# Attention with a small state and a gated MLP on one core: x of batch 0 in 2 KB pieces, its state read in 64x32 tiles in one visit

## The chip, the core and the metric

The kernel runs on one core of a Trainium2 chip. The metric is the device time of one execution in microseconds (us). The core's engines run side by side and meet only at semaphores: TensorE (PE in the profile, with its weight loads as PEld), VectorE (DVE), ScalarE (ACT), GpSimd (POOL) and SyncE (SP), whose queue issues nearly all transfers here. 16 DMA engines move the bytes.

## The reference

`x` is [8, 8, 512, 64] (batch, head, token, feature) and `state` is [8, 8, 32, 64], all in float32. Tokens read from the state, the state reads from the tokens, and both results go through one MLP:

```
scores  = x @ state^T / 8;  a  = softmax(scores)       # over the 32 states
xread   = a @ state                                    # 512 rows of a head
scores2 = state @ x^T / 8;  a2 = softmax(scores2)      # over the 512 tokens
sread   = a2 @ x                                       # 32 rows of a head
attn    = concat([xread, sread], rows)                 # 544 rows of a head
X       = heads side by side                           # [8 * 544, 512]
out     = mish(X @ w_in) @ w_out                       # 512 -> 2048 -> 512
```

In the code the state read (`sread`) is the product of the exponentials `e2` with x; `rs` holds the reciprocals of their sums.

## The kernel before, in words

The weights are loaded as 32-bit words, put together and split into a high and a low float32r part; the products of the MLP are sums of three float32r matmuls. `w_in` is folded with the state of a batch first (`sw`, psum `swp`), so that the attention's read and the first layer are one product (`ph`). Mish of it is `g`, split into `gh` and `gl`, and the second layer accumulates in `acc`.

Batch 0 is the prologue. While the weights still arrive, its attention, the preparation of all weights and its MLP are interleaved by a list of steps that is written out by hand. Each step is a generator: every mention in the list runs it up to its next `yield`, so one step has two or three parts on different engines. PE, DVE and ACT each execute their instructions in the order of that list. Afterwards the batches 1 to 7 run in a loop of eight slots each, with the attention of the next batch in between; there DVE and ACT are ordered by the planner, and PE still in the order of the code.

The transfers go out on SP's queue in program order, mostly chained behind one another: the four pieces of x of batch 0 first (256 KB each, a pair of heads, line 124), then `w_in` and `w_out` by turns (`wir`, line 173, and `wor`, line 185). The state of batch 0 (`sn`) goes out on ACT's queue at the same time.

These steps of the list carry what follows (all of batch 0, all recorded under line 66, the helper that issues them):

- `x0` to `x3`: four PE transposes of a pair of heads into a bank (`xTp`), then a copy to SBUF (`xT`), by ACT for pairs 0 and 2, by DVE for 1 and 3. `st` (psum `st`) transposes the state on PE by products with the identity, `sc` makes the scores, `scs` their scaled copy.
- `tr`, `ex`, `no`, `pr`: the softmax over the states, up to `ah` and `al`, the operands of the first layer. `p0` to `p7` are the first layer's products, `m0` to `m7` their Mish on ACT and the split on DVE, `g0` to `g7` the second layer.
- `hi`, `ci`, `di`, `ji` put the words of `w_in` together, `ho`, `co`, `do`, `jo`, `lo` those of `w_out`, on ACT and DVE; `sw0` to `sw7` fold `w_in` on PE (`swp`), copied to `swh` by ACT and `swl` by DVE.
- `ee0`, `ee1`: the exponentials `e2` of the two halves of the heads (a half is one head of each pair, kc = 0 or 1; 128 rows are 4 heads x 32 states), first on ACT, then the sums' reciprocals on DVE.
- `et0`, `et1`: the first part is on PE, four transposes of 128x128 of half kc into a bank `e2p`; the second is on ACT, the copy to `e2T`.
- `sr0`, `sr1`: the first part is on PE, 16 float32 matmuls for half kc (four token groups x four heads, each 128 tokens deep, 32 states by 64 features) into a bank `srp`; the second is on DVE, the scaling to `srd`.

The order around them is this stretch of the list; between the first parts of `et1` and `sr0` there is no other PE work, and on ACT the Mish of `m3` is ahead of the second part of `et1`:

```
... sw3 ee0 g1 g1 sw3 et0 m2 ee1 ci4 co3 sw3 et0 p3
m2 jo2 et1 lg2 lo2 m3 et1 sr0 ho3 g2 ji4 sw4 ho5 sr0 g2 g2 g2 sr1 jo3 sw4 ... sr1 p4
```

`e2p`, `srp`, `swp` and `xTp` share the two banks of the pool `misc`. A float32 matmul that isn't a transpose is executed as two passes, and the profile counts both.

Of the kernel before, what the change touches and what calls it, by code (L numbers as in the profile page):

```python
# [9 lines left out]
F32 = mybir.dt.float32  # L10
# [7 lines left out]
P = 128  # L18
B, H, S, NS, D = 8, 8, 512, 32, 64
# [29 lines left out]
def half(par):  # L49
    return slice(par * D, (par + 1) * D)  # L50
# [23 lines left out]
def state_attention_mish_kernel(ctx, tc, x, state, w_in, w_out, out):  # L74
# [11 lines left out]
    def misc(name):  # L86
        return ps_m.tile([P, 512], F32, tag="m", name=name)

    def spare(b):


        return misc if b < 2 else first_bank
# [7 lines left out]
    def temp(name, shape=(P, S)):  # L100
        return pool.tile(list(shape), F32, tag="t", name=name, bufs=5)
# [13 lines left out]

    def load_x(b):

        shape = [P, NC, 2, NT * D]
        if b == 0:
            xs = const.tile(shape, F32, tag="wo7", name="x_0")  # L120
        else:
            xs = pool.tile(shape, F32, tag="x", name=f"x_{b}", bufs=1)
        for c in range(NC):
            last["load"] = nc.sync.dma_start(  # L124
                xs[:, c], x[b].rearrange("(c k) (p t) d -> c p k (t d)", k=2, t=NT)[c])
        return xs
# [129 lines left out]
    def attention(b, sn, xq=None):  # L256
# [4 lines left out]
        def x_transposed(c):  # L261

            if xq is not None:
                xTs[c] = temp(f"xT_{b}_{c}")
                dve.transpose(
                    xTs[c].rearrange("p (k v i g) -> p g k v i", k=2, v=2, g=4),
                    xq[:, c].rearrange("p k (g v) d -> p g k v d", v=2))
                return
            pt = (first_bank if b == 0 and c > 1 else misc)(f"xTp_{b}_{c}")
            for i in range(NT):  # L270
                pe.transpose(
                    pt[:, i * P:(i + 1) * P], xss[b][:, c, i // 2, (i % 2) * P:(i % 2 + 1) * P], ident)
            yield
            xTs[c] = temp(f"xT_{b}_{c}")
            if b == 0 and c % 2:
                dve.tensor_copy(xTs[c], pt)
            else:
                act.copy(xTs[c], pt)

        def scores():  # L280

# [39 lines left out]
        def soft2_e(kc):  # L321
            e2 = temp(f"e2_{b}_{kc}")
            sm = pool.tile([P, 1], F32, tag="sm", name=f"sm_{b}_{kc}")
            act.activation(e2, sc[kc], AF.Exp, bias=nms[kc], accum_out=sm)
            yield
            dve.tensor_scalar_add(sm, sm, 1e-9)
            rs2[kc] = pool.tile([P, 1], F32, tag="rs", name=f"rs_{b}_{kc}", bufs=4)
            dve.reciprocal(rs2[kc], sm)
            e2s[kc] = e2

        def e2_transposed(kc):
            e2 = e2s[kc]
# [49 lines left out]
        def soft1_n():  # L382
            sums, turned = ([small[kc][i] for kc in two] for i in (1, 2))

            def total(kc):
                dve.tensor_reduce(sums[kc], groups(e1[kc]), AX.X, ALU.add)

            def guard(kc):
                dve.tensor_scalar_add(sums[kc], sums[kc], 1e-9)

            def turn(kc):
                dve.reciprocal(turned[kc], sums[kc])

            def norm(kc):
                dve.tensor_mul(groups(e1[kc]), groups(e1[kc]), wide(turned[kc]))

            for step, kc in ((total, 0), (guard, 0), (total, 1), (turn, 0), (guard, 1), (norm, 0)):
                step(kc)
            yield
            turn(1)  # L400
            norm(1)
# [21 lines left out]

        def sread(kc):

            if b == 0 or kc == 0:
                srd["bank"] = misc(f"srp_{b}_{kc}") if b == 0 else spare(2)(f"srp_{b}")
            pr = srd["bank"][:, :D] if b == 0 else srd["bank"][:, kc * D:(kc + 1) * D]
            for t in range(NT):
                for h4 in range(4):  # L430
                    o = slice(h4 * NS, (h4 + 1) * NS)
                    last["PE"] = pe.matmul(
                        pr[o],
                        e2T[kc][:, t, o],
                        xss[b][:, h4, kc, t * D:(t + 1) * D],
                        start=(t == 0), stop=(t == NT - 1),
                    )
            yield
            if kc == 0 and b == 0:
                srd[0] = pool.tile([P, 2, D], F32, tag="srd", name=f"srd_{b}", bufs=1)  # L440
            dve.tensor_scalar_mul((srds[0][:, b - 1] if b else srd[0])[:, kc], pr, rs2[kc])

        def sreadT():
            pt = misc(f"srTp_{b}")[:, :P]
# [7 lines left out]

        own = dict(
            x=x_transposed, st=lambda _: state_blocks(b, sn) if b else state_blocks_0(sn), sc=lambda _: scores(), tr=soft1_t, ex=soft1_x,
            no=lambda _: soft1_n(), pr=soft1_a, mm=soft2_m, ee=soft2_e, et=e2_transposed, sr=sread,
            rt=lambda _: sreadT(), fill=fill, aT=aT)

        def soft2():
# [114 lines left out]
    def gemm2(key, fcs, gh, gl, ntok, ts=None):  # L573

        if key not in accs:
            new_accs(key, ntok)
        for t in ts or range(ntok):

            parts = (slice(0, 256), slice(256, 512)) if (key, fcs[-1], t) == (B - 1, NFC - 1, ntok - 1) else (slice(0, 512),)
            for part in parts:  # L580
                for i, fc in enumerate(fcs):
                    col = (i * ntok + t) * P
                    sl = slice(col, col + P)
                    ops = [(gh, 1), (gh, 0), (gl, 1)]
                    for n, (g, w) in enumerate(ops):
                        last["PE"] = pe.matmul(
                            accs[key][t][:, part], g[:, sl], wo[fc // 2][:, fc % 2, w, part],
                            start=(fc == 0 and n == 0), stop=(fc == NFC - 1 and n == 2),
                            skip_group_check=part.start > 0,
                        )  # L590
            if len(parts) > 1:
                for part, engine in zip(parts, (act.copy, dve.tensor_copy)):
                    o = pool.tile([P, 256], F32, tag="e2T", name=f"o_{key}_{t}_{part.start}")
                    engine(o, accs[key][t][:, part])
                    (nc.scalar if part.start else nc.sync).dma_start(
                        out[key * T:key * T + S, part].rearrange("(p t) e -> p t e", t=NT)[:, t, :], o)
            elif fcs[-1] == NFC - 1:
                o = pool.tile([P, DM], F32, tag="o", name=f"o_{key}_{t}")
                if t % 2 == 0:
                    dve.tensor_copy(o, accs[key][t])  # L600
                else:
                    act.copy(o, accs[key][t])
                if key == "s":
                    for b4 in range(4):
                        r0 = (4 * t + b4) * T + S
                        nc.sync.dma_start(out[r0:r0 + NS, :], o[b4 * NS:(b4 + 1) * NS, :])
                else:
                    last["store"] = nc.sync.dma_start(
                        out[key * T:key * T + S, :].rearrange("(p t) e -> p t e", t=NT)[:, t, :], o)


    raws, rawo, wfull = {}, {}, {}
# [62 lines left out]
    for step in """  # L675
            x0 x0 x1 x1 st st x2 x2 x3 x3 sc acc sc sc sc sc ci0 tr0 tr1 hi0 tr0 tr0 ex0 tr1 tr1 fill2
            ex1 ci1 ji0 sw0 no sw0 sw0 fill2 no hi1 pr0 ho0 pr0 ji1 pr1 pr1 co0 fill2 pr0 pr1 sw1 jo0
            sw1 p0
            m0 ho1 fill6 jo0 sw1 hi2 m0 lo0 lg0 p1
            do1 di2 ji2 jo1 g0 g0 sw2 mm0 m1 hi4 sw2 hi3 jo1 g0 sw2 ci3 lo1 m1 lg1 g0 p2  # L680
            g1 ji3 g1 ho2 mm1 do2 jo2 ee0 ee1 sw3 ee0 g1 g1 sw3 et0 m2 ee1 ci4 co3 sw3 et0 p3
            m2 jo2 et1 lg2 lo2 m3 et1 sr0 ho3 g2 ji4 sw4 ho5 sr0 g2 g2 g2 sr1 jo3 sw4 m3 sw4 jo3 ci5 ho4
            hi5 hi6 co5 lo3 sr1 p4
            co4 ji5 sw5 sw5 lg3 ST g3 m4 sw5 g3 jo4 X1 jo4 p5
            lo4 rt X1 X2 ci6 g3 rt m4 ji6 lg4 X0 rt X2 m5 X0 X3 sw6 X3 jo5 jo5 sw6 co6 lo5 g3 SC g4 sw6
            m5 SC lg5 SC TR0 ho6 TR0 g4 p6
            EX0 TR1 TR1 g4 jo6 g4 ci7 hi7 EX1 ji7 g5 g5 ho7 m6 sw7 jo6 sw7 NO NO g5 sw7 m6 PR0 g5 next
            p7
            lo6 lg6 co7 g6 next g6 m7 next jo7 PR1 PR1 jo7 PR0 g6 m7 PR1 PR0 lo7 lg7 g6
            """.split():  # L690
        what, i = re.fullmatch(r"([a-zA-Z]+)(\d*)", step).groups()
        if not hasattr(begun.get(step), "send"):
            begun[step] = steps[what](int(i or 0))
        if hasattr(begun[step], "send"):
            next(begun[step], None)
# [123 lines left out]
```

## Time and profile before

| what | value |
|---|---|
| median of 3 runs | 660.15 us (659.8 to 661.0) |
| profiled execution, first to last instruction | 657.8 us |
| PE busy | 648.9 us, 99% of the span |
| DVE, ACT busy | 338.2 us, 259.0 us |
| chain that ended last | PE 96%, DMA 1%, DVE 1%, ACT 1%, SP's queue 1% |
| granted TensorE clock | 1.000 |

For the profiled execution only its span is recorded; the timed runs lie 2.0 to 3.2 us above it, for what precedes the first and follows the last instruction. Busy time is the union of an engine's instructions; matmuls overlap, so their rows start closer together than they last. In a timeline row the columns are start, duration, engine, line, operation, output and inputs, tile, shapes and count, and in brackets the idle time before it and what ended it. A tile such as 64*32 is the part of the PE array that a matmul takes, rows by columns.

### The profile page before, as it was taken

To read this page: it belongs to the slowest core of one execution; us is meant where nothing else is said; L and a number is where in the kernel's file an instruction comes from. 1 tells how busy PE (TensorE), PEld (TensorE's weight loads), DVE (VectorE), ACT (ScalarE), POOL (GpSimd) and SP (SyncE) were. 2 spreads that over 40 slices of the span, in tenths; PEclk is the share of its full clock that TensorE was granted. 3 is DMA by queue.
4 is the path that set the end of the run, shared out by engine and by line. 5 is a ranking of instruction groups with operands and counts; after the bars stand their busy time and mean duration, and the time that the engine had idled before them with its cause. 6 is when DMAs were issued, how large, how long until landed. Compare 5 with 4: busy or idle time off the path is not lost.

```text
span 657.8 us, 10837 instructions
## 1 busy us (share of the span) xinstructions
PE 648.9 (99%) x4556; PEld 519.9 (79%) x4556; DVE 338.2 (51%) x518; ACT 259.0 (39%) x411; POOL 0.7 (0%) x6
## 2 busy tenths in 40 slices
PE   8999999999999999999999999999999999999997
PEld 5777677777778877787778887787778899878886
DVE  4979994356447345654437245544537345232222
ACT  4988753245315313442325222532235334131110
POOL 0000000000000000000000000000000000000000
PEclk9999999999999999999999999999999999999999
DMA  8975303400034002310033003400110001000001
GB/s 325 409 246 194 48 15 88 106 9 1 33 71 99 1 1 77 80 45 2 33 78 92 1 1 90 104 9 1 50 49 32 1 1 65 0 17 18 1 0 64
DMA packets 80672, 42.05 MB, mean 64 GB/s; under 512 B 61808, under 2 KB 70256, under 8 KB 80624
## 3 DMA queue, kind: packets, MB, share of 16 engines
q1 hardware_dynamic: 80192, 41.18, 21.6%
q8 instruction: 35, 0.57, 0.4%
q10 hardware_dynamic: 432, 0.20, 0.1%
q14 instruction: 13, 0.11, 0.0%
HBM read 32.44 MB, written 8.91 MB: 63 GB/s over the span
## 4 chain that ended last, share of the span: by engine, by line
PE 96%; DMA 1%; DVE 1%; ACT 1%; SPq 1%; issue 0%; ACTq 0%
PE acc L66 54%; PE ph L66 26%; PE swp L66 5%; PE ph_s L66 3%; PE acc_s L66 3%; DMA wir<-in_moe_w_in_dram 1%; PE srp L66 1%; PE sc L66 1%; PE e2p L66 1%; SPq L124 0%; SPq L173 0%; ACT wir L66 0%; DVE w_in_sb L66 0%; DVE gl L66 0%; ACT xT L66 0%
## 5 line engine op out<-in xcount | busy, mean ns | idle before, releaser
L66 PE MATMUL acc<-wo,gh 128*128 128x512 f32 (+1 forms) x1028 | 320.4, 393 | 0.0
L66 PEld LDWEIGHTS acc<-wo,gh 128*128 128x128 f32 x1028 | 189.8, 188 | 47.0 <-issue 8.6
L66 PE MATMUL acc<-wo,gl 128*128 128x512 f32 (+1 forms) x514 | 199.8, 389 | 0.0
L66 ACT ACTIVATE g<-ph 128x512 f32<-128x512 f32 x128 | 72.4, 597 | 198.0 <-DVE gl L66 172.9
L66 PEld LDWEIGHTS acc<-wo,gl 128*128 128x128 f32 x514 | 96.5, 188 | 20.4
L66 DVE CAST gh<-g 128x1024 fp32r<-128x1024 f32 x64 | 43.6, 682 | 114.0 <-PE acc L66 109.8
L66 DVE TENSOR_TENSOR gl<-g,gh 128x1024 fp32r<-128x1024 f32 x64 | 78.3, 1223 | 4.9 <-DVE sm L66 0.4
L66 PE MATMUL ph<-ah,swh 128*128 128x512 f32 x256 | 79.2, 392 | 0.0
L66 PE MATMUL ph<-al,swh 128*128 128x512 f32 x256 | 78.6, 389 | 0.0
L66 PE MATMUL ph<-ah,swl 128*128 128x512 f32 x256 | 78.5, 389 | 0.0
L66 DVE TENSOR_TENSOR swl<-swp,swh 128x512 fp32r<-128x512 f32 (+1 forms) x72 | 41.1, 624 | 68.5 <-ACT swh L66 68.4
L66 PEld LDWEIGHTS ph<-al,swh 128*128 128x128 f32 x256 | 48.0, 188 | 10.1
L66 PEld LDWEIGHTS ph<-ah,swl 128*128 128x128 f32 x256 | 48.1, 188 | 10.1
L66 PEld LDWEIGHTS ph<-ah,swh 128*128 128x128 f32 x256 | 47.6, 188 | 10.5 <-ACT ah L66 0.4
L66 ACT ACT_TABLE_LOAD x35 | 44.9, 1283 | 16.5 <-DVE gl L66 14.9
L66 ACT CAST swh<-swp 128x512 fp32r<-128x512 f32 (+1 forms) x72 | 34.3, 549 | 38.5 <-PE swp L66 38.5
L66 PE MATMUL swp<-w_in_sb,bd 64*32 64x256 f32 x1024 | 34.5, 381 | 0.4 <-ACT xT L66 0.2
L66 PEld LDWEIGHTS swp<-w_in_sb,bd 64*32 64x32 f32 x1024 | 17.4, 106 | 13.6 <-issue 7.7
L66 DVE TENSOR_REDUCE nm<-scs 128x1 f32<-128x512 f32 x16 | 10.3, 677 | 34.7 <-ACT scs L66 34.7
L66 DVE STREAM_TRANSPOSE xT<-xq 128x512 f32<-128x512 f32 x24 | 24.1, 1067 | 3.1 <-PE e2p L66 3.1
L66 ACT COPY o<-acc 128x512 f32<-128x512 f32 (+1 forms) x16 | 9.2, 574 | 41.8 <-PE acc L66 37.4
L66 DVE COPY o<-acc 128x512 f32<-128x512 f32 (+1 forms) x17 | 11.4, 670 | 21.6 <-PE acc L66 15.9
(84 smaller groups left out, 473.3 us busy)
## 6 DMA issues: line engine op xcount, KB each, us to landing
x<-in_x_dram SPq DMA_DIRECT2D x32, 256.0 KB, 4.1
wir<-in_moe_w_in_dram SPq DMA_DIRECT2D x16, 512.0 KB, 9.0
wor<-in_moe_w_out_dram SPq DMA_DIRECT2D x16, 512.0 KB, 8.1
out_dram<-o SPq DMA_DIRECT2D x31, 256.0 KB, 2.4
xq<-in_x_dram SPq DMA_DIRECT2D x192, 32.0 KB, 2.3
sn<-in_state_dram SPq DMA_DIRECT2D x28, 32.0 KB, 2.1
out_dram<-o_s SPq DMA_DIRECT2D x8, 64.0 KB, 1.7
out_dram<-o SPq DMA_DIRECT2D x1, 128.0 KB
```

Of the source, the lines that this page charges most:

```text
L66: made = method(*args, **kwargs)
```

## The change

It touches batch 0 alone. A row of x now holds eight consecutive tokens of one head (2 KB), and the 128 rows of a piece hold the two heads of a pair, 64 rows each; before, a row held four tokens of each of the two heads, in two pieces of 1 KB. The copies to `xT` put the columns in the new order, which leaves the scores' layout as it was. Since a head's tokens are now on 64 rows, the exponentials are transposed so that the two halves kc lie on rows 0 to 63 and 64 to 127 (`e2_transposed_0`, products with the identity, two visits), and the state read runs both halves in one visit, with 64 rows by 32 columns for each matmul (`sread_0`). The two copies of `e2` are announced one part earlier. The step `sr1` is gone from the list. The output rows of batch 0 are stored with two transfers a tile in place of one.

```diff
     def load_x(b):
         if b == 0:
-            xs = const.tile(shape, F32, tag="wo7", name="x_0")
+            xs = const.tile([P, NC, 2 * NT * D], F32, tag="wo7", name="x_0")
+            for c in range(NC):
+                last["load"] = nc.sync.dma_start(
+                    xs[:, c], x[b].rearrange("(c k) (q t) d -> c (k q) (t d)", k=2, t=2 * NT)[c])
+            return xs
...
     def x_transposed(c):
+                xi = xss[b][:, c, i * P:(i + 1) * P] if b == 0 else xss[b][:, c, i // 2, (i % 2) * P:(i % 2 + 1) * P]
+                pe.transpose(pt[:, i * P:(i + 1) * P], xi, ident)
...
+            if b == 0:
+                to, pt = to.rearrange("d (k i q) -> d k i q", k=2, i=NT), pt.rearrange("d (i k q) -> d k i q", k=2, i=NT)
...
     def soft2_e(kc):
+            e2s[kc] = e2
             yield
...
-            e2s[kc] = e2
+        def e2_transposed_0(i):
+            pt = misc(f"e2p_{b}_{i}")
+            for t in range(NT):
+                for kc in range(2):
+                    n = (i * NT + t) * D
+                    pe.matmul(
+                        pt[half(kc), t * P:(t + 1) * P], e2s[kc][:, n:n + D], ident, start=True, stop=True)
+            yield
+            e2T[i] = pool.tile([P, NT, P], F32, tag="e2T", name=f"e2T_{b}_{i}")
+            act.copy(e2T[i].rearrange("p t n -> p (t n)"), pt)
+
+        def sread_0():
+            prs = [misc(f"srp_{b}_{kc}")[:, :D] for kc in range(2)]
+            for i in range(2 * NT):
+                v, u, w = i // 4, i // 2 % 2, i % 2
+                t = 4 * v + 2 * w + u
+                for h4 in range(4):
+                    o = slice(h4 * NS, (h4 + 1) * NS)
+                    for kc in range(2):
+                        last["PE"] = pe.matmul(
+                            prs[kc][o], e2T[i // NT][half(kc), i % NT, o], xss[b][half(kc), h4, t * D:(t + 1) * D],
+                            start=(i == 0), stop=(i == 2 * NT - 1))
+            yield
+            srd[0] = pool.tile([P, 2, D], F32, tag="srd", name=f"srd_{b}", bufs=1)
+            for kc in range(2):
+                dve.tensor_scalar_mul(srd[0][:, kc], prs[kc], rs2[kc])
...
     def gemm2(...):                                   # the store of a finished tile t
+                    if key == 0:
+                        to = to.rearrange("(q v w u) e -> v u w q e", v=2, w=2, u=2)[t // 2, t % 2]
+                        for w in range(2):
+                            last["store"] = nc.sync.dma_start(to[w], o[half(w)])
...
-            m2 jo2 et1 lg2 lo2 m3 et1 sr0 ho3 g2 ji4 sw4 ho5 sr0 g2 g2 g2 sr1 jo3 sw4 m3 sw4 jo3 ci5 ho4
-            hi5 hi6 co5 lo3 sr1 p4
+            m2 jo2 et1 lg2 lo2 m3 et1 sr0 ho3 g2 ji4 sw4 ho5 sr0 g2 g2 g2 jo3 sw4 m3 sw4 jo3 ci5 ho4
+            hi5 hi6 co5 lo3 p4
```

More of the change, by code (lines that the diff above doesn't have):

```diff
@@ L116, in load_x @@
     def load_x(b):
-        shape = [P, NC, 2, NT * D]
         if b == 0:
-            xs = const.tile(shape, F32, tag="wo7", name="x_0")
-        else:
-            xs = pool.tile(shape, F32, tag="x", name=f"x_{b}", bufs=1)
+            xs = const.tile([P, NC, 2 * NT * D], F32, tag="wo7", name="x_0")
[3 more added lines that the diff above has]
+            return xs
+        xs = pool.tile([P, NC, 2, NT * D], F32, tag="x", name=f"x_{b}", bufs=1)
         for c in range(NC):
@@ L270, in x_transposed @@
             for i in range(NT):
-                pe.transpose(
-                    pt[:, i * P:(i + 1) * P], xss[b][:, c, i // 2, (i % 2) * P:(i % 2 + 1) * P], ident)
+                xi = xss[b][:, c, i * P:(i + 1) * P] if b == 0 else xss[b][:, c, i // 2, (i % 2) * P:(i % 2 + 1) * P]
+                pe.transpose(pt[:, i * P:(i + 1) * P], xi, ident)
             yield
             xTs[c] = temp(f"xT_{b}_{c}")
+            to = xTs[c]
+            if b == 0:
+                to, pt = to.rearrange("d (k i q) -> d k i q", k=2, i=NT), pt.rearrange("d (i k q) -> d k i q", k=2, i=NT)
             if b == 0 and c % 2:
-                dve.tensor_copy(xTs[c], pt)
+                dve.tensor_copy(to, pt)
             else:
-                act.copy(xTs[c], pt)
+                act.copy(to, pt)
         def scores():
@@ L424, in sread @@
         def sread(kc):
-            if b == 0 or kc == 0:
-                srd["bank"] = misc(f"srp_{b}_{kc}") if b == 0 else spare(2)(f"srp_{b}")
-            pr = srd["bank"][:, :D] if b == 0 else srd["bank"][:, kc * D:(kc + 1) * D]
+            if kc == 0:
+                srd["bank"] = spare(2)(f"srp_{b}")
+            pr = srd["bank"][:, kc * D:(kc + 1) * D]
             for t in range(NT):
@@ L438, in sread @@
             yield
-            if kc == 0 and b == 0:
-                srd[0] = pool.tile([P, 2, D], F32, tag="srd", name=f"srd_{b}", bufs=1)
-            dve.tensor_scalar_mul((srds[0][:, b - 1] if b else srd[0])[:, kc], pr, rs2[kc])
+            dve.tensor_scalar_mul(srds[0][:, b - 1, kc], pr, rs2[kc])
         def sreadT():
@@ L454, in attention @@
             x=x_transposed, st=lambda _: state_blocks(b, sn) if b else state_blocks_0(sn), sc=lambda _: scores(), tr=soft1_t, ex=soft1_x,
-            no=lambda _: soft1_n(), pr=soft1_a, mm=soft2_m, ee=soft2_e, et=e2_transposed, sr=sread,
+            no=lambda _: soft1_n(), pr=soft1_a, mm=soft2_m, ee=soft2_e, et=e2_transposed if b else e2_transposed_0,
+            sr=sread if b else lambda _: sread_0(),
             rt=lambda _: sreadT(), fill=fill, aT=aT)
@@ L607, in gemm2 @@
                 else:
-                    last["store"] = nc.sync.dma_start(
-                        out[key * T:key * T + S, :].rearrange("(p t) e -> p t e", t=NT)[:, t, :], o)
+                    to = out[key * T:key * T + S, :]
+                    if key == 0:
+                        to = to.rearrange("(q v w u) e -> v u w q e", v=2, w=2, u=2)[t // 2, t % 2]
+                        for w in range(2):
+                            last["store"] = nc.sync.dma_start(to[w], o[half(w)])
+                    else:
+                        last["store"] = nc.sync.dma_start(to.rearrange("(p t) e -> p t e", t=NT)[:, t, :], o)
     raws, rawo, wfull = {}, {}, {}
```

## The prediction

> **What bounds the kernel now.** I read the page first, then the busy time by stage, the waits, and the chain of the prologue. The page's span and its chain by engine:
>
> ```profile
> span 657.8 us, 10837 instructions
> PE 96%; DMA 1%; DVE 1%; ACT 1%; SPq 1%; issue 0%; ACTq 0%
> ```
>
> The busy time by stage says where PE has room: 4.48 us of idle time in the first 20 us, none in the long loop. Columns are PE, PEld, DVE, ACT, POOL, clock, DMA share and GB/s.
>
> ```profile
> 10.00:15.00 5.00, 4.38 (x32) 2.44 (x32) 4.31 (x8) 3.52 (x6) 0.00 (x0) 1.00 1.04 408
> ...
> sum 20.00, PE 15.52 PEld 10.30 DVE 11.03 ACT 11.41 POOL 0.70; mean PE 3.88 PEld 2.58 DVE 2.76 ACT 2.85 POOL 0.18
> ```
>
> ```profile
> 120.00:640.00 520.00, 520.00 (x3692) 421.35 (x3691) 243.77 (x378) 175.85 (x291) 0.00 (x0) 1.00 0.15 36
> ```
>
> PE's waits from 19 to 130 us are one line:
>
> ```profile
> PE swp L66 <- ACT xT L66: 0.2, 1, 0.2
> ```
>
> So from about 20 us on, each us added to PE's stream moves the end by one us. Before that the chain is another: it runs through the loads.
>
> ```profile
> 5.44 9.40 DMA wir<-in_moe_w_in_dram
> ...
> 14.92 0.33 ACT wir L66
> ...
> 15.96 0.37 ACT swh L66
> ...
> 16.35 0.75 DVE swl L66 x2
> ```
>
> ACT waits for the second piece of `w_in` (landed at 14.84), and `swh`, `swl` and the second half of the softmax queue up behind it. DVE is free for `swl` from 16.00 (next fence), so if the loads alone came earlier the gain would stop at 16.35 - 16.00 = 0.35. The other path to that point, x itself, waits too: PE's second transposes stand idle for 0.64 until their piece has landed.
>
> ```profile
> 15.31 0.69 DVE L66 TENSOR_TENSOR e<-e,r 128x512 f32<-128x512 f32 x1
> ```
>
> ```profile
> 4.95 0.72 PEld L66 LDWEIGHTS xTp<-ident,x 128*128 128x128 f32 x4 [0.64 <-PE xTp L66]
> ```
>
> **The change, part by part.** *Loading x (A).* The three stretches here are the ramp (1.8 to 2.6 us), x alone (4.2 to 5.2) and 2 KB pieces of `w_in` (6.4 to 8.0); columns are packets, MB, share of 16 engines.
>
> ```profile
> q1 hardware_dynamic: 139, 0.14, 52.8%
> ```
>
> ```profile
> q1 hardware_dynamic: 339, 0.33, 103.3%
> ```
>
> ```profile
> q1 hardware_dynamic: 299, 0.58, 98.3%
> ```
>
> A 1 KB packet takes 1.0 x 16 x 1.033 / 339 = 48.8 ns of an engine, a 2 KB one 1.6 x 16 x 0.983 / 299 = 84.2 ns. x is 1024 of the first, 3.12 us on 16 engines, or 512 of the second, 2.69 us: all loads behind x come 0.43 earlier. The x path has its 0.64 of waiting to give, so both paths move. Bounds: 0, if what ends last is an uneven engine, and -0.8, if the ramp, idle for 47% of its 0.8 us (0.38), were limited by the number of packets as well. I take A = -0.43.
>
> The Trainium skill ("DMA: Bandwidth & Descriptors", Specifications) gives 512 B as the least transfer for line rate. By it, pieces of 1 KB and of 2 KB go equally fast and A is 0; the two rows differ by 14% per byte. It is a rival below.
>
> The copies to `xT` take 64 columns at a time in a new order. The nearest copy with such an order is `bd`, 32 columns at a time:
>
> ```profile
> 6.72 0.42 DVE L66 COPY bd<-st 128x256 f32<-128x256 f32 x1
> ```
>
> 0.42 for 256 columns lies beside 0.59 for 512 straight ones on ACT (`xT` below); I take no cost, with 0.25 (2 x 0.42 - 0.59) for the last copy as the upper bound.
>
> *Transposing the exponentials (B).* The PE stream around both visits:
>
> ```profile
> 41.89 0.39 PE L66 MATMUL acc<-wo,gl 128*128 128x512 f32 x1
> ...
> 43.02 0.63 PE L66 MATMUL ph<-al,swh 128*128 128x512 f32 x2
> 43.49 0.62 PE L66 MATMUL ph<-ah,swl 128*128 128x512 f32 x2
> ...
> 44.87 0.62 PE L66 MATMUL ph<-ah,swl 128*128 128x512 f32 x2
> 45.33 0.60 PE L66 MATMUL e2p<-ident,e 128*128 128x128 f32 x4
> 45.86 0.65 PE L66 MATMUL srp<-x,e2T 128*32 128x64 f32 x32
> 46.44 0.74 PE L66 MATMUL acc<-wo,gh 128*128 128x512 f32 x2
> 47.02 0.39 PE L66 MATMUL acc<-wo,gl 128*128 128x512 f32 x1
> ```
>
> The large matmuls start 0.233 apart (43.02 to 43.49 is two). `et0` costs 43.02 - 41.89 less three steps, 0.43: four passes of 0.108 for 128 columns. The new visit has eight products with the identity, each counted twice, on half of the array's columns. Such a visit is in the trace:
>
> ```profile
> 5.99 0.68 PE L66 MATMUL st<-ident,sn 128*64 128x128 f32 x8
> ```
>
> One after the other, eight passes would need 0.86 and the last one's end; they run in pairs. So 16 passes are eight rounds, 0.87. A change of the tile shape comes on top:
>
> ```profile
> 47.71 0.39 PE L66 MATMUL acc<-wo,gl 128*128 128x512 f32 x1
> 48.03 0.66 PE L66 MATMUL swp<-w_in_sb,bd 64*32 64x256 f32 x16
> ...
> 49.18 0.40 PE L66 MATMUL acc<-wo,gl 128*128 128x512 f32 x1
> ```
>
> `swp` costs 1.47 - 0.70 = 0.77, of which 16 passes of 256 columns, eight at a time, are 0.43: 0.34 for the change of shape and back. B = 0.87 + 0.34 - 0.43 = +0.78.
>
> *The second transposes, the new wait and the read (C).* Before, `sr0` needed only the first copy, long done; PE went from `e2p` to `srp` directly. Now the read takes both halves at once, and its second bank is the one that the second `e2p` leaves, so PE waits for the second copy on ACT. That copy stands behind the Mish of `m3`:
>
> ```profile
> 45.34 1.09 ACT L66 ACTIVATE g<-ph 128x512 f32<-128x512 f32 x2 [0.31 <-ACT e2T L66]
> 46.31 0.59 ACT L66 COPY e2T<-e2p 128x512 f32<-128x512 f32 x1
> ```
>
> From a copy's end to its use on PE (7.88 to 7.93) passes 0.05:
>
> ```profile
> 7.29 0.59 ACT L66 COPY xT<-xTp 128x512 f32<-128x512 f32 x1 [1.96 <-PE xTp L66]
> ```
>
> ```profile
> 7.93 0.14 PEld L66 LDWEIGHTS sc<-xT,bd 64*32 64x32 f32 x4 [0.15 <-ACT xT L66]
> ```
>
> In the times of before, with B: the last `ph` starts at 45.10 + 0.78 = 45.88; `e2p` starts 0.32 later (as 47.71 to 48.03), at 46.20, its last round at 46.96, and ends at 47.24 (a pass lasts 0.60 - 3 x 0.108 = 0.28). The second Mish, which needs the last `ph` (45.88 + 0.39), is out of the way by 46.9. The copy ends at 47.85, PE starts the read at 47.90, where it would have been free at about 47.15: a wait of 0.75.
>
> The read has 128 passes of 64 columns (0.054 each by 0.108 for 128) on eighths of the array. In rounds of eight that is 16 x 0.054 = 0.87, as much as the two old visits of eight rounds of four. That eight passes can start within 0.054 is seen at `swp`, where 16 weight loads take 0.18 together:
>
> ```profile
> 48.02 0.18 PEld L66 LDWEIGHTS swp<-w_in_sb,bd 64*32 64x32 f32 x16 [0.36 <-issue]
> ```
>
> The way back costs 0.58 - 0.43 = 0.15 (45.86 to 46.44), so `acc` restarts at 47.90 + 0.87 + 0.15 = 48.92, and the third matmul, 47.02 before, at 49.50: +2.48 with B, so C = +1.70. Bounds: 0.95 without the wait; 2.57, if the halves don't run side by side (another 0.87).
>
> *The visit that goes (D).* `sr1` stood alone between two large blocks:
>
> ```profile
> 52.62 0.39 PE L66 MATMUL acc<-wo,gl 128*128 128x512 f32 x1
> 52.94 0.65 PE L66 MATMUL srp<-x,e2T 128*32 128x64 f32 x32
> ...
> 54.10 0.39 PE L66 MATMUL ph<-al,swh 128*128 128x512 f32 x1
> ```
>
> D = -(1.48 - 0.70) = -0.78.
>
> *At no cost.* ACT's work behind the copy moves by some 0.9 (47.85 against 46.90), and with it DVE's `w`:
>
> ```profile
> 49.38 1.23 DVE L66 SCALAR_TENSOR_TENSOR w<-wor 128x1024 uint32<-128x1024 uint32 x1 [2.00 <-ACT wor L66]
> ```
>
> PE itself is 2.48 late there and 1.70 after `sr1`'s place, more than either, which is the cover; without it up to 0.9 would be paid. Both scalings of the read fall into DVE's idle 2.00. `swp` needs both banks of the read, but 1.27 us of matmuls lie between (46.44 to 47.71). The four more stores on SP's queue push batch 3's pieces of x back; at 16.49 / 24 = 0.69 an issue that is under 3 us, and they are read 60 us later:
>
> ```profile
> 108.19 16.49 SPq L137 DMA_DIRECT2D xq<-in_x_dram  x24
> ```
>
> ```profile
> 171.52 1.99 DVE L66 STREAM_TRANSPOSE xT<-xq 128x512 f32<-128x512 f32 x2
> ```
>
> **The sum.** A + B + C + D = -0.43 + 0.78 + 1.70 - 0.78 = +1.27. The profiled span goes from 657.8 to 659.1; the median lies 2.35 above the span, so 660.15 + 1.27 = 661.4. By the skill's 512 B it would be 661.8.
>
> **The rivals.**
> 1. *Hardly slower: the loads were held back by more than packet time.* From 2 to 6 us, nearly all of it x, the queues moved
>
> ```profile
> DMA packets 1397, 1.19 MB, mean 297 GB/s; under 512 B 351, under 2 KB 1347, under 8 KB 1397
> ```
>
> At the 408 GB/s of 10 to 15 us that takes 2.9 in place of 4.0; with the ramp's 0.38 A is up to -1.5, the sum +0.2 and the time 660.35. For it: the ramp. Against: x's own path has only 0.64 of waiting to give. From A = -1.70 on it would be no loss.
> 2. *The wait isn't paid*, because work that the trace hides fills it: 661.4 - 0.75 = 660.7. Against: the list's order, with nothing for PE in between.
> 3. *Slower: the read doesn't do what it says.* The row halves don't overlap at 64 columns, 661.4 + 0.87 = 662.3. For: no row has such a shape with 64 columns; against: `swp`.
> 4. *Slower: a floor per pass.* The 32 passes of `srp` take 0.58, 18 ns each; if that is a floor and not the array's time, 128 passes take 2.3 in place of 0.87, 662.8. Against: the weight loads of `swp`. The Trainium skill states such a floor, 25 ns from start to start ("TensorE: Matmul & The Clock Gate", Part 1); by it the read would take 3.2 and the time be 663.7, but `srp` is already below it.
> 5. *A = 0*, both sizes equally fast: 661.8.
> 6. *Faster by over 1.3 us.* PE's idle 4.48 at the start would have to shrink by 3.0; the loop, with PE busy 520.00 of 520.00, has nothing to give to another plan.
>
> **How the numbers follow.** 0.2% of the time, 1.32 us, is about what a measurement tells from no change; the forecast lies just inside. Forecast 0.47 (slower 0.20, same 0.27), rival 1 0.13 and rival 2 0.08 (same), rival 3 0.08, rival 5 0.12 and rival 4 0.05 (slower), rival 6 0.07. So faster 0.07, same 0.48, slower 0.45. The range runs from rival 1 with some of rival 2 (660.1) to rival 3 with some of A lost (662.6) and leaves out rivals 4 and 6; the forecast's own is 660.9 to 661.9.
>
> **What would show it.** A: the load that ends at 14.84 in the chain ends at about 14.4, and all behind it starts 0.4 earlier. B: 16 passes of `e2p` a visit, 128*64, `et0` at 1.2 net. C: an idle stretch of about 0.75 before `srp`, ended by ACT's `e2T`, then 128 passes within about 1.1. D: one visit of `srp`. The prediction is wrong if the gap before `srp` is small, if the first 20 us shrink by over 1 us, or if PE gets idle time after 50 us that it had not before.

## The result: slower by 0.24%, and the profile after

The changed kernel takes 662.12 us (median of 22 runs, 660.98 to 664.61) against 660.6 of the kernel before on the same chip: a ratio of 1.0024, 95% interval 1.0016 to 1.0033, or +1.6 us (1.06 to 2.18). The forecast was 661.4, +1.27. Direction and most steps were right; one term was 0.43 too hopeful, one 0.46 too cheap. The 1.27 itself lies inside the timed interval, so what was off is read from the rows, not from the time.

The page and the busy time by stage say where to look. PE lost 0.46 us of busy time between 40 and 60 us, and nothing in the long loop (columns: PE, PEld, DVE, ACT, POOL, clock, DMA share, GB/s). The first row of the second block below is the kernel before, the other two are the changed one.

```profile
span 660.3 us, 11016 instructions
...
PE 650.8 (99%) x4644; PEld 521.5 (79%) x4644; DVE 338.3 (51%) x518; ACT 259.2 (39%) x411; POOL 0.7 (0%) x6
```

```profile
40.00:60.00 20.00, 20.00 (x175) 14.89 (x174) 15.30 (x24) 19.55 (x26) 0.00 (x0) 1.00 0.55 194
...
40.00:60.00 20.00, 19.54 (x254) 14.54 (x253) 13.30 (x22) 17.79 (x24) 0.00 (x0) 1.00 0.43 144
...
120.00:640.00 520.00, 520.00 (x3693) 421.42 (x3692) 243.78 (x378) 176.65 (x293) 0.00 (x0) 1.00 0.15 37
```

PE's waits from 19 to 130 us have one new line:

```profile
PE srp L66 <- ACT e2T L66: 0.5, 1, 0.5
PE swp L66 <- ACT xT L66: 0.2, 1, 0.2
```

The PE stream around both transposes and the read, to be held against the same stretch of before:

```profile
42.19 0.39 PE L66 MATMUL acc<-wo,gl 128*128 128x512 f32 x1
42.51 1.09 PE L66 MATMUL e2p<-ident,e 128*64 128x128 f32 x16
43.53 0.73 PE L66 MATMUL ph<-ah,swh 128*128 128x512 f32 x2
44.11 0.62 PE L66 MATMUL ph<-al,swh 128*128 128x512 f32 x2
...
45.93 0.61 PE L66 MATMUL ph<-ah,swl 128*128 128x512 f32 x2
46.48 1.09 PE L66 MATMUL e2p<-ident,e 128*64 128x128 f32 x16
47.50 0.30 PE L66 MATMUL srp<-x,e2T 64*32 64x64 f32 x2
48.26 1.47 PE L66 MATMUL srp<-x,e2T 64*32 64x64 f32 x126 [0.46 <-ACT e2T L66]
49.66 0.73 PE L66 MATMUL acc<-wo,gh 128*128 128x512 f32 x2
50.23 0.40 PE L66 MATMUL acc<-wo,gl 128*128 128x512 f32 x1
```

Two passes of the read slip in at 47.50, because the first `e2T` is long there; the third needs the second `e2T` and starts at 48.26. The wait list shows 0.46, since those two passes last 0.30; by the starts the read is held up for 0.76, from 47.50 to 48.26. ACT's rows say what it waits for: the second Mish of `m3`, then PE's last transposes, then the copy.

```profile
46.59 0.61 ACT L66 ACTIVATE g<-ph 128x512 f32<-128x512 f32 x1 [0.34 <-PE ph L66]
47.62 0.59 ACT L66 COPY e2T<-e2p 128x512 f32<-128x512 f32 x1 [0.43 <-PE e2p L66]
```

The copy starts 0.43 after the Mish has made room, so with this order it is PE's `e2p` and the copy's own 0.59 that PE waits for, not the Mish.

The experiments need a mark that does not feel the loads: the distance from the first Mish of batch 0 to its first copy of an output tile. Rows of before, then of after:

```profile
22.52 1.09 ACT L66 ACTIVATE g<-ph 128x512 f32<-128x512 f32 x2
```

```profile
98.40 0.68 DVE L66 COPY o<-acc 128x512 f32<-128x512 f32 x1
```

```profile
22.80 1.08 ACT L66 ACTIVATE g<-ph 128x512 f32<-128x512 f32 x2
```

```profile
100.74 0.68 DVE L66 COPY o<-acc 128x512 f32<-128x512 f32 x1
```

That is 75.88 before and 77.95 after (from the trace's starts, in ns): +2.06. From there on the two traces run side by side: the last copy of an output lies 555.66 behind the first in both (555.63 to 555.89 in all runs below). Each distance is that of one execution. In some executions of every timed kernel TensorE runs at half its clock for about 3.4 us near 20 us, which makes them 1.4 to 2.1 us longer; leaving these out, the mean time is 661.66 after and 659.79 to 659.93 before, +1.7 to 1.9 (by the spans +2.0 to 2.1), and the mark starts behind that place.

### The profile page after: what moved, and what is told of

The parts are those of the page before. It is cut to its first block, busy times and chain, and to the rows that moved or that the text cites. A ratio compares the mean times of both kernels' runs of the same rounds, so it can differ in the third digit from the quotient of the medians.

```text
span 660.3 us, 11016 instructions
## 1 busy us (share of the span) xinstructions
PE 650.8 (99%) x4644; PEld 521.5 (79%) x4644; DVE 338.3 (51%) x518; ACT 259.2 (39%) x411; POOL 0.7 (0%) x6
## 4 chain that ended last, share of the span: by engine, by line
PE 96%; DMA 1%; ACT 1%; SPq 1%; DVE 1%; issue 0%; ACTq 0%
PE acc L66 54%; PE ph L66 26%; PE swp L66 5%; PE ph_s L66 3%; PE acc_s L66 3%; DMA wir<-in_moe_w_in_dram 1%; PE srp L66 1%; PE e2p L66 1%; PE sc L66 1%; SPq L122 0%; SPq L176 0%; SPq L188 0%; DVE w_in_sb L66 0%; ACT wir L66 0%; DVE gl L66 0%
```

## The experiments

`e6` and `e7` ran once each; the others were timed in 11 or 12 executions beside the kernel before, on the same chip. "Net" below is what a visit costs PE beyond the large matmuls around it (their starts are 0.23 apart).

**One part alone: the load.** The kernel before, with only the 2 KB load of x; it computes batch 0 on permuted tokens and heads.

```diff
+            if b == 0:
+                last["load"] = nc.sync.dma_start(
+                    xs[:, c].rearrange("p k f -> p (k f)"),
+                    x[b].rearrange("(c k) (q t) d -> c (k q) (t d)", k=2, t=2 * NT)[c])
+                continue
```

> The kernel before with the new load of x of batch 0 alone (2 KB pieces); nothing else follows the new layout, so batch 0 computes on tokens and heads in another order. Two marks: the first Mish of batch 0 (22.53 us before, 22.80 after in the profiles) for the start, and from there to the first copy of an output tile (98.41 and 100.75) for the rest of batch 0, 75.88 before and 77.95 after. Theory: the rest stays at 75.9 within 0.1; the loads come earlier, the start mark at about 22.1 and the time 0.4 us shorter (ratio 0.9994). Rival 1, both piece sizes equally fast: 22.5 and 1.0000. Rival 2, the later landing seen in the profile after is the new load's own: 22.8 and 1.0004.

Measured: ratio 1.0002 (0.999 to 1.0014), distance 75.90, the first Mish at 22.47 (22.52 before), and ACT starts on the second piece of `w_in` at 14.87 (14.92 before):

```profile
14.87 1.15 ACT L66 ACTIVATE wir<-wir 128x1024 uint32<-128x1024 uint32 x1 [0.53 <-DMA wir<-in_moe_w_in_dram]
```

The interval of the ratio holds all three expectations. Without the executions at half clock the mean span is 657.85 against 657.74, with standard errors of 0.14 and 0.08: +0.11, which leaves no room for a gain of 0.43. So A is 0 as far as can be told. The reason is in the stretch from 4.2 to 5.2 us, x alone; first the changed kernel, then this one:

```profile
q1 hardware_dynamic: 173, 0.31, 99.1%
```

```profile
q1 hardware_dynamic: 176, 0.32, 106.3%
```

A 2 KB packet of x takes 1.0 x 16 x 0.991 / 173 = 91.7 ns, or 96.6 ns, 1.9 to 2.0 times the 48.8 of a 1 KB packet. PE's wait for the second piece of x does vanish from the waits of the first 19 us (0.3 before), but nothing behind it comes earlier.

**The read one tile later**, behind one more tile of the second layer, so that the second `e2T` is there; `sw4` had to move as well.

```diff
-m3 et1 sr0 ho3 g2 ji4 sw4 ho5 sr0 g2 g2 g2 jo3
+m3 et1 ho3 g2 sr0 ji4 g2 sw4 ho5 sr0 g2 g2 jo3
```

> The changed kernel with the read of the state one tile of the second layer later, so that PE has 1.4 us of work while ACT copies the second transposes (the next step that needs the two banks is moved one tile too). Theory: the wait of 0.76 goes, from the first Mish to the first output copy 77.2 in place of 77.95, ratio to before about 1.0013. Rival, the wait hides something that comes due elsewhere: 77.95 and 1.0024.

Measured: ratio 1.0024 (1.0011 to 1.0037), distance 77.67. A miss: the wait is gone from PE's list, yet only 0.27 of its 0.76 came back. Part of the rest is in the chain, where behind the moved `sw4` the work of ACT and DVE becomes the end; `e10`, further down, leaves `sw4` in its place and is 0.22 shorter, and what is missing there has another reason.

```profile
51.12 1.41 PE srp L66 x91
...
54.12 0.70 PE swp L66 x16
...
55.45 1.04 ACT wir L66
56.49 1.03 ACT wor L66
```

**Joint exponentials, single-pass transposes.** Both halves' exponentials go into one tile, so that a transpose of 128x128 takes both; the 16 passes on half columns become four whole ones.

```diff
-                for kc in range(2):
-                    pe.matmul(pt[half(kc), t * P:(t + 1) * P], e2s[kc][:, n:n + D], ident, ...)
+                pe.transpose(pt[:, t * P:(t + 1) * P], e2s["both"][:, n:n + P], ident)
```

> The changed kernel with both halves' exponentials written side by side into one tile (columns group, half, token), so that one 128x128 transpose turns both halves: four single-pass transposes a visit, as before, in place of 16 passes on half the columns. Theory: the first visit gets cheap again (0.43 in place of 1.22); the second too, but there the wait for ACT grows to 1.09, because ACT's Mish is in the way; from the first Mish to the first output copy 77.0 (before 75.88, after 77.95), ratio to before 1.0010. Rival, the two-pass transposes were hidden by that wait throughout: 77.9.

Measured: distance 76.98, as expected, but ratio 1.0022 (1.001 to 1.0034), with the expected 1.0010 at the edge of the interval. The first visit costs 0.42 net again (1.22 with the change), so B is undone in the trace. The wait grows, since PE is done earlier; here the copy does stand behind the Mish, and starts at 48.17 with no idle time on ACT before it:

```profile
47.17 0.60 PE L66 MATMUL e2p<-ident,e 128*128 128x128 f32 x4
47.70 0.30 PE L66 MATMUL srp<-x,e2T 64*32 64x64 f32 x2
48.81 1.47 PE L66 MATMUL srp<-x,e2T 64*32 64x64 f32 x126 [0.82 <-ACT e2T L66]
```

The read behind it takes as long as before, 48.81 to 50.21: neither the transposes' shape nor the wait's length bears on it. Without the executions at half clock, the mean span is 1.67 above that of the kernel before, the distance only 1.10; why is open. A cleaner pair for the gain is `e8` and `e10` below, which differ by the joint exponentials alone: 1.29 in the distance, 1.34 in the spans.

**Both**, joint exponentials and the read one tile later (the two edits above together).

> Both: transposes of the joint exponentials, and the read one tile later. Theory: no wait and no extra passes; one read of 1.25 and one change of shape in place of two reads of 0.45 and two changes, 75.9 from the first Mish to the first output copy, as before the change. The time against before is then what the load alone does (0.9994 by the theory of an earlier load, 1.0000 otherwise). Rival, a cost not found yet: over 76.3.

Measured: ratio 1.0009 (0.9998 to 1.002), distance 76.31, 0.4 over the theory and at the bound that its rival names. Again the chain from 51.28 to 66.6 runs through `swh` on ACT and the weights' words, not through PE; this time it gets there by the landing of a piece of `w_in` at 51.27. So the order has to be changed without moving `sw4`; against `e8`, which does that, the move is worth 0.15 of the 0.4.

**The read where `sr1` stood**, with `sw4` in its old place and the transposes as in the change.

```diff
-m3 et1 sr0 ho3 g2 ji4 sw4 ho5 sr0 g2 g2 g2 jo3 ... lo3 p4
+m3 et1 ho3 g2 ji4 sw4 ho5 g2 g2 g2 sr0 jo3 ... lo3 sr0 p4
```

> The changed kernel with only the read put there, the transposes in two passes left as they are. Theory: the wait of 0.76 goes and nothing else, 77.2 from the first Mish to the first output copy (after 77.95), ratio 1.0016. Rival, the wait's end is not free, since ACT and DVE are late anyway: 77.7 or more, as in the version one tile later.

Measured: ratio 1.0022 (1.0008 to 1.0036), distance 77.45; between the two expectations. The wait is gone, and 0.50 of its 0.76 came back. The stream says where the rest is:

```profile
46.75 0.61 PE L66 MATMUL ph<-ah,swl 128*128 128x512 f32 x2
47.30 1.09 PE L66 MATMUL e2p<-ident,e 128*64 128x128 f32 x16
48.32 0.73 PE L66 MATMUL acc<-wo,gh 128*128 128x512 f32 x2
48.89 0.39 PE L66 MATMUL acc<-wo,gl 128*128 128x512 f32 x1
...
54.50 0.39 PE L66 MATMUL acc<-wo,gl 128*128 128x512 f32 x1
54.82 1.48 PE L66 MATMUL srp<-x,e2T 64*32 64x64 f32 x128
56.23 0.73 PE L66 MATMUL ph<-ah,swh 128*128 128x512 f32 x2
56.80 0.40 PE L66 MATMUL ph<-al,swh 128*128 128x512 f32 x1
```

The second transposes cost 48.89 - 46.75 - 4 x 0.23 = 1.22 alone and the read 56.80 - 54.50 - 3 x 0.23 = 1.60 alone, 2.82 together; in the change both with the wait between them cost 50.23 - 45.93 - 0.92 = 3.38. The 0.56 between them is the wait less one more change of the tile shape in and out (0.20). The read itself, 54.82 to 56.23, takes 1.41 with no wait ahead of it.

**Joint exponentials and the read where `sr1` stood.**

> The changed kernel with the joint exponentials and the one read put where the second read of the kernel before stood (behind three tiles of the second layer), so that the next step that needs the two banks keeps its place. Theory: the run with the read one tile later lost 0.4 because that step moved with it and ACT and DVE came late; here nothing moves, so from the first Mish to the first output copy 75.9 (before 75.88; the version one tile later 76.31) and the ratio to before 1.000. Rival: the 0.4 is the read's own (its slow passes and one more thing not found), 76.3 and 1.0006.

Measured: ratio 0.9999 (0.9986 to 1.0011), distance 76.16, between the two expectations and 0.28 over before. With the new transposes and the wait both out, the net costs are 0.44 for `et0`, 0.63 for `et1` alone and 1.60 for the read, 2.67 in all; before they are 0.43, 1.22 for `et1` and `sr0` together and 0.78 for `sr1`, 2.43. So the single read of 128 passes, by itself, does not pay for the visit that it saves. The timed ratio does not tell this run from the kernel before.

**Is it one visit or the new shape?** The kernel before, with its two reads one behind the other in that place.

```diff
-m3 et1 sr0 ho3 g2 ji4 sw4 ho5 sr0 g2 g2 g2 sr1 jo3 ... lo3 sr1 p4
+m3 et1 ho3 g2 ji4 sw4 ho5 g2 g2 g2 sr0 sr1 jo3 ... lo3 sr0 sr1 p4
```

> The kernel before with its two reads one behind the other at that place (no new layout, no new load). Theory: one change of the tile shape less, 0.34: 75.55 from the first Mish to the first output copy, ratio 0.9995, the only part of the change that is a gain. Rival: a visit's cost is not the change of shape, 75.9 and 1.0000.

Measured: ratio 0.9992 (0.9978 to 1.0006), which holds both expectations; distance 75.75, a little nearer to the rival. Its read:

```profile
51.74 0.39 PE L66 MATMUL acc<-wo,gl 128*128 128x512 f32 x1
52.06 1.10 PE L66 MATMUL srp<-x,e2T 128*32 128x64 f32 x64
53.09 0.73 PE L66 MATMUL ph<-ah,swh 128*128 128x512 f32 x2
53.66 0.62 PE L66 MATMUL ph<-al,swh 128*128 128x512 f32 x2
```

53.66 - 51.74 - 3 x 0.23 = 1.22 net, for the same sums that cost 1.60 on 64x32 tiles. One visit in place of two is good for 0.13 of the distance; the smaller tiles cost 0.38. It has the shortest distance of all kernels here, but its time isn't told apart from that of the kernel before.

**The read in two visits of 64 passes**, one tile of the second layer between them (the loop of `sread_0` yields after its fourth round; `sw4` moves as in `e2`).

> The changed kernel with the read in two visits of 64 passes, a tile of the second layer (1.4 us) between them. In the profile of the changed kernel the first 34 passes start 7 ns apart and the rest 10. Theory, PE's instructions are supplied at 10 ns a pass and a store of about 34 passes fills while PE waits or has long matmuls: each visit begins with some 34 fast passes. Rival, the later token groups are slow for where their data lie: the second visit is slow from its first pass. Either way the first visit still waits for ACT; from the first Mish to the first output copy 78.1.

Measured once: distance 78.51, 0.4 over the expectation; the chain goes through ACT again from 53.95, as in `e2`, which may be what the 0.4 is. The visits:

```profile
48.45 0.84 PE L66 MATMUL srp<-x,e2T 64*32 64x64 f32 x62 [0.46 <-ACT e2T L66]
49.22 0.73 PE L66 MATMUL acc<-wo,gh 128*128 128x512 f32 x2
...
50.80 0.86 PE L66 MATMUL srp<-x,e2T 64*32 64x64 f32 x64
```

By the starts of single passes, the first 32 of the second visit start within 0.24 (50.80 to 51.04, most of them 7 ns apart), the other 32 take 0.40. In the change's one visit, too, some 34 passes go at 7 ns, and the last 92 take 0.93 (48.58 to 49.51), 10.1 ns each on average. So the passes 65 to 96, slow in the change, are fast here: what counts is how many passes lie behind the last break, not which data they read.

**Every pass of the read twice.** The flag `start=(i == 0)` stays in the code, so the second time through begins the sum anew: it comes out as before, not twice as large as the expectation says.

```diff
-            for i in range(2 * NT):
+            for i in (*range(2 * NT), *range(2 * NT)):
```

> The changed kernel with every matmul of the state read of batch 0 issued twice in its one visit (256 passes of 64 columns on 64x32 tiles; the sum of batch 0's read comes out twice as large). In the changed kernel the passes of this read start 7 ns apart for the first 34 or so and 10 ns apart after that. Theory (PE's supply of instructions gives out: a short stock is used up at the fast rate, and from then on a pass costs 10 ns whatever it reads): the added 128 passes all start 10 ns apart, the visit is 1.3 us longer, and the distance from the first Mish to the first copy of the output goes from 77.95 to 79.2. Rival (the pace hangs on which tokens and which part of the exponentials are read, so the repetition starts as fast as the first time): the added passes show a second stretch of some 30 passes 7 ns apart, the visit is 1.1 to 1.2 us longer, the distance is 79.1 and the stretch is to be seen in the starts. Rival (the array's own time, 0.054 a round of eight, with one stall somewhere): the added 128 passes take 0.87, the distance is 78.8.

Measured once: 668.46, distance 84.78. All three theories missed, by a stop that none of them has:

```profile
47.04 0.30 PE L66 MATMUL srp<-x,e2T 64*32 64x64 f32 x2
47.80 1.89 PE L66 MATMUL srp<-x,e2T 64*32 64x64 f32 x171 [0.46 <-ACT e2T L66]
53.52 1.06 PE L66 MATMUL srp<-x,e2T 64*32 64x64 f32 x83 [3.83 <-issue]
```

Up to the stop the first theory holds: the 45 added passes before it start 10 ns apart on average, with no second fast stretch. Then, after 173 passes, PE stands still for 3.83 us and waits for nothing that the profile shows. In that gap (51 to 52 us) the queue that carries instructions moves its one packet of the stretch:

```profile
q8 instruction: 1, 0.02, 5.8%
```

What that queue carries is seen in its totals, in the kernel before, the changed kernel and this run:

```profile
q8 instruction: 35, 0.57, 0.4%
...
q8 instruction: 36, 0.59, 0.4%
...
q8 instruction: 37, 0.61, 0.4%
```

PE executes 9112, 9288 and 9544 matmuls and weight loads in these three, so there is one packet of 16 KB to every 258 to 260 of them, and the 256 added here bring one packet more, while the counts of ACT and DVE stay the same. The packets are PE's instructions. Between the packet at 34.42 and the one at 51.22, PE had started 525 when it stopped; between the same two packets they are 485 in the changed kernel and 264 in the kernel before. The packet of the gap has landed at 52.15, and PE goes on at 53.52.

Then the passes start as at the beginning: 32 within 0.24 (53.52 to 53.76), the rest slower. After the idle time the clock also comes down, for 3.4 us from 55.1 on (columns as above):

```profile
54.50:57.00 2.50, 2.50 (x21) 1.56 (x22) 2.21 (x4) 0.00 (x0) 0.00 (x0) 0.62 0.02 7
```

Of the 6.83 beyond 77.95, 3.83 are this gap; the rest are the added passes and the stretch at a clock of 0.62.

So two things have to be kept apart. The stop is a lack of instructions, as far as the counts and the order of events show it; no run here made them arrive earlier. The pace of 10 ns has another cause: in the changed kernel no packet of that queue moves between 36.4 and 52.2, so the read at 48 to 50 runs on instructions that were already there, and its pace is the same in every run. It hangs on how many passes lie behind the last break (`e7`), not on the data (`e6`, `e7`), and it is above the array's time of the first rounds. A limit on how fast PE takes up small instructions fits; no run here varies it, and the cause stays open.

## Why the prediction was right or wrong

- **What bounds the kernel: right.** From 20 us on PE's stream sets the end. Net costs and the distance agree in each kernel on the old order of `sw4`: +2.17 by the rows and +2.06 by the mark for the change against before; -1.04 and -0.97 for `e3` and -0.57 and -0.50 for `e10`, against the change; +0.24 and +0.28 for `e8` and -0.13 and -0.13 for `e9`, against before.
- **A, -0.43: wrong, it is 0.** The step that failed is the price of a 2 KB packet, 84.2 ns, taken from pieces of `w_in` in another stretch of time. x's own take 91.7 to 96.6, and even that stretch of `w_in` is at 1.6 x 16 x 1.041 / 293 = 91.0 in the changed kernel:

```profile
q1 hardware_dynamic: 293, 0.58, 104.1%
```

  The row varies by 8% from one execution to another, and the forecast rested on a difference of 14%. Rival 5 was right. By the Trainium skill ("DMA: Bandwidth & Descriptors", Specifications) a transfer needs 512 B for line rate; here pieces of 1 KB and of 2 KB go about equally fast per byte, which agrees. The load that was to end at 14.4 released ACT at 15.21 in the changed kernel and at 14.87 in `e1` (14.92 before): no gain in either. One trace could not have shown 0.43 in any case: the piece lands between 14.25 and 15.79 in the nine profiled executions with the new load, and at 14.44 and 14.84 in the two with the old one.
- **B, +0.78: right.** `et0` costs 44.11 - 42.19 - 0.70 = 1.22 in place of 0.43, +0.79; `e3` gives it back in its rows, and `e8` against `e10` in the time as well.
- **C, the wait of 0.75: right.** 0.76 by the starts, ended by ACT's copy, with rival 2 out: nothing fills it.
- **C, the read: too cheap.** 0.87 and 0.15 for the way back were put down; 48.26 to 49.66 is 1.40, +0.38. The mis-sized term is the round of eight passes, 0.054 by the array's time alone: it holds for the first four rounds (0.056) and not beyond. The sign that it gave, 128 passes within about 1.1, was missed too: the last 126 alone take 1.25 from first start to last. Rival 3 (halves one after the other, 1.74) is out, and rival 4's 18 ns is too; but its idea, a limit per pass, is what happens from about the 34th pass on, at 10 ns. The 25 ns from start to start of the Trainium skill ("TensorE: Matmul & The Clock Gate", Part 1) are no floor for these passes, which lie 10 or 7 ns apart on different tiles of the array. A further 0.07 went into the second transposes (1.02 against 0.95). Together C is 3.38 - 1.22 = +2.16, not +1.70.
- **D, -0.78: right.** One visit of `srp` is gone, and its passes are in C.
- **The sum.** 0 + 0.79 + 2.16 - 0.78 = +2.17, against +2.06 in the traces and +1.6 (1.06 to 2.18) timed. The two errors, 0.43 in A and 0.46 in C, went the same way and make up the 0.9 between 1.27 and 2.17; the timed interval, 1.06 to 2.18, holds both 1.27 and 2.17 and does not choose between them. That the time came out near the forecast is in part the width of this interval: 662.12 is inside the stated range (660.1 to 662.6) but above the 660.9 to 661.9 that the prediction called the forecast's own.
- **At no cost: right.** No new wait on PE but the one named, and the copies to `xT` in the new order take 0.59 on ACT and 0.69 on DVE, as before.

## What to carry to other kernels

An edit that halves the number of visits can lose by what it asks to be ready at once: look for the copy that becomes the last input, and for what stands ahead of it on its engine. Price a transfer from the same buffer and the same stretch, or give it the spread of the row between executions. And cost a burst of very small matmuls by a stretch as long as itself: the starts of 32 passes say nothing of the 128th.

## What the runs showed of the hardware that was not expected

- Matmul passes on 64x32 tiles with 64 columns start 7 ns apart for some 32 to 34 passes after a break, and 10.1 ns apart on average from then on (change), again 32 after 1.6 us of large matmuls (`e7`). In the starts of the weight loads the slower pace is a pause of 79 and 55 ns after the 33rd, and one of about 34 ns after the 68th, the 102nd and, in `e6`, the 136th and 170th. The Trainium skill gives TensorE's queue a depth of 64 ("TensorE: Matmul & The Clock Gate", Part 1); 32 passes with their 32 weight loads are 64, which fits, but no run here varies it.
- PE stood still for 3.83 us after a burst of 173 such passes, with 525 matmuls and weight loads started since the last packet of its instructions, and went on 1.4 us after the next had landed (`e6`).
- The half clock near 20 us, here in an execution of `e3` (columns as above):

```profile
20.00:22.50 2.50, 2.50 (x20) 1.82 (x6) 2.18 (x4) 2.48 (x4) 0.00 (x0) 0.51 1.05 419
```

  PE had idled for 1.73 us in one piece before it, waiting for the softmax. The length of that idle time does not decide by itself: in `e10` the clock fell after 1.28 us, while `e7` with 1.61 us and the changed kernel with 1.55 us kept their clock of 1.00. The Trainium skill ("TensorE: Matmul & The Clock Gate", Part 1) puts the fall after an idle window of about 3.4 us. Here less sufficed, in a quarter to a half of the executions of each timed kernel, the kernel before included (19 of 64).
